# The last scattered output tile of an attention–Fourier–FFN kernel: one store of 768 columns, or two of 384

## The chip, the cores and the metric

The kernel runs on one core of a Trainium2 chip. The metric is device time in microseconds (us) for one execution of the whole program. Engines are named by their role: TensorE (PE in the profile, with its weight loads as PEld), VectorE (DVE), ScalarE (ACT), GpSimd (POOL) and SyncE (SP). DMA transfers are issued from SyncE's queue and from GpSimd's queue, and all run on the same 16 DMA engines.

## The reference

Attention with normalised queries and keys, then a Fourier mix, a layer norm and a feed-forward block, for 8 batches of 448 rows and 768 columns:

```python
batch, n_heads, seq, head_dim = (8, 12, 448, 64)
...
scores = np.matmul(q_n, k_n.transpose(0, 1, 3, 2)) / tau
attn = np.exp(scores - max); attn = attn / sum
x = np.matmul(attn, v)            # heads side by side: (8, 448, 768)
...
X = np.fft.fft(np.fft.fft(x, axis=1), axis=2)
u = x + np.real(X)
un = (u - mu) / np.sqrt(var + 1e-06)
ch = np.maximum(un @ w_ch1, 0.0) @ w_ch2        # 768 -> 3072 -> 768
return (u + ch).astype(np.float32)
```

The output is float32: one row is 768 numbers, 3 KB.

## The kernel before

The program is written as a list of operations (`Plan.add`), each with its engine, an estimated duration, a priority, and the names of what it reads and writes. A list scheduler (`Plan.schedule`) puts them into one fixed order for each engine, and `Plan.emit` writes that order out with the semaphore waits that the reads and writes need. Two rules of `emit` matter here. On GpSimd each instruction waits for the semaphore of the instruction before it, and an indirect store raises that semaphore too (`engine_sem`). An instruction that must wait for a transfer waits for that transfer's own semaphore, `st0`, `st1`, `st1z` for the direct stores from SyncE and `sx0`, `sx1` for the indirect stores from GpSimd. At the end SyncE waits for all of these, and then every engine drains and they meet in a barrier (line L1571 in the profile).

The 448 rows of a batch are held in tiles of 128 rows (`utiles`): A0 has rows in their natural order, A1 has mirrored rows, Yt has rows 128 and on with a mirrored piece, and Zt collects 64 mirrored rows of an even batch and 64 of the odd batch after it. A0 is stored by a direct DMA from SyncE (L1378). The other tiles go to rows that are not evenly spaced, so GpSimd stores them by an indirect DMA (L1386) that takes the 128 row numbers from a column of the table `IDX` ([128, 8 batches, 3 kinds of tile], int32). `IDX` is filled once, at the start of the program, by `iota` instructions on GpSimd (L551 to L556). The column of kind 2 (Zt) is used for the odd batches alone.

`ffn(b)` computes the second matrix product and the stores. It takes two row tiles u0 and u1 at a time, and gets the four output halves (two tiles by two halves of 384 columns) from seven products m1 to m7 of 12 matmuls each. For the last batch (`last_b`) the second pair is u0 = Zt, with output buffer 0, and u1 = A0, with buffer 1. In order of time on the engines:

- m1: ScalarE copies it from PSUM into half 0 of buffer 0 (L1352), GpSimd adds the residual tile to it in two instructions of 192 columns (L1357).
- m2: VectorE adds it from PSUM to half 0 of buffer 0 (L1364, called `fin{i}0`): half 0 of u0 is complete.
- m6, m5: copied by ScalarE and added to by GpSimd in the same way, into half 1 of buffer 0 and half 1 of buffer 1 (two pairs of L1357).
- m7: VectorE completes half 1 of u1 (L1364); SyncE stores it. VectorE also prepares the last 128 columns of u1 (L1464), which the next products wait for.
- m3: VectorE completes half 1 of u0 (L1364, `fin{i}1`); then GpSimd stores all 768 columns of u0.
- m4, in two parts of 256 and 128 columns: VectorE completes half 0 of u1 (L1364, L1470); SyncE stores it in two parts.

So the indirect store of Zt (u0) and the last direct store of A0 (u1) are the last things that leave the core.

Of the kernel before, what the change touches and what calls it, by code (L numbers as in the profile page):

```python
# [12 lines left out]
B, H, S, DH = 8, 12, 448, 64  # L13
# [394 lines left out]
def t_dve(n, mode=1):  # L408
    return 0.1 + n / (960.0 * mode)
# [15 lines left out]
class Kern:  # L425
# [943 lines left out]
    def store(self, b, i, ut, ob, c=None, c0=0, c1=384):  # L1369

        P = self.P
        A0, A1, Yt, Zt, zo = self.utiles(b)
        rd_ = [f"OUT{ob}", f"OUT{ob}b"] if c is None else [f"OUT{ob}" + "b" * c + "z" * (c0 > 0)]
        cs = slice(0, DM) if c is None else slice(384 * c + c0, 384 * c + c1)
        o = self.OUTB[:, ob, cs]
        if ut == A0:
            n = cs.stop - cs.start
            op = P.add("sp", lambda sy, sem: sy.dma_start(  # L1378
                bass.AP(self.out.tensor, b * S * DM + cs.start, [[DM, 128], [1, n]]), o).then_inc(sem, 16),
                0.36, -1, f"st{i}_{b}", reads=rd_, dma=(f"st{ob}" + "z" * (c0 > 0), 16), serve=1.2)  # L1380
            self.first_st = self.first_st or op
        else:
            w = {A1: 0, Yt: 1, Zt: 2}[ut]

            def st(g, sem, esem):
                g.indirect_dma_start(  # L1386
                    self.out.rearrange("b s d -> (b s) d"),
                    bass.IndirectOffsetOnAxis(self.IDX[:, b, w:w + 1].bitcast(mybir.dt.uint32), 0),
                    o, None, engine_sem=esem).then_inc(sem, 16)
            P.add("pool", st, 1.2, -1, f"sc_{i}_{b}", reads=rd_ + ["IDX"], dma=(f"sx{ob}", 16), serve=1.2)  # L1390

    def ffn(self, b):
        P = self.P
        tiles = self.tiles(b)
        HH = NF // 2
        if b == 0:
            self.up(0, (0,), range(0, NF, 4), False)
            self.up(0, (1, 2), range(0, NF, 2), True)
            for i, ut in enumerate(tiles):
                ob = self.out_next % 2  # L1400
# [23 lines left out]
        def comb(o, a, bq, k, op, nm):  # L1424
            cs = lambda q: self.HQ[:, q, 4 * k:4 * k + 4, :].rearrange("p f c -> p (f c)")
            rd = sorted(set(hr(a)(k) + hr(bq)(k)))
            P.add("dve", lambda v: v.tensor_tensor(cs(o), cs(a), cs(bq), op), 0.46, -0.5, f"{nm}{k}_{b}", reads=rd, writes=hr(o)(k))  # L1427
        last_b = b == self.nb - 1
        for i, two in ((0, 0), (1, 1)) if b == self.nb - 2 else [(i, i + 1 < len(tiles)) for i in range(0, len(tiles), 2)]:
            if two:  # L1430
                u0, u1 = tiles[i], tiles[i + 1]
                if b >= self.nb - 2:
                    if not last_b:
                        self.wsum3()
                    self.ups(b, (i, i + 1))
                else:
                    self.up(b, (i, i + 1), chunks, True)
                for k in range(3):
                    comb(4, 2, 3, k, AluOp.add, "s1")
                    comb(2, 2, 0, k, AluOp.subtract, "s3")  # L1440
                b1, ta, tb = Tile("M"), Tile("M"), Tile("G" if last_b else "M")
                op = self.prod(b, b1, H(0), W(0, 0), hr(0), wr(0), f"m1{i}", True, False)
                rd = self.fin(b, b1, op, 0, 0, u0, "a", f"fa{i}")
                for k in range(3):
                    comb(0, 4, 0, k, AluOp.subtract, "s2")
                op = self.prod(b, ta, H(1), W(1, 0), hr(1), wr(1), f"m2{i}", True, True)
                self.fin(b, ta, op, 0, 0, u0, "out", f"fin{i}0")
                for k in range(3):
                    comb(1, 1, 0, k, AluOp.subtract, "s4")
                op = self.prod(b, b1, H(0), TT(1), hr(0), tr(2), f"m6{i}", False, False, rd)  # L1450
                rd = self.fin(b, b1, op, 0, 1, u0, "a", f"fv{i}")
                op = self.prod(b, tb, H(4), TT(0), hr(4), tr(1), f"m5{i}", True, False)
                rd2 = self.fin(b, tb, op, 1, 1, u1, "a", f"fm{i}")
                op = self.prod(b, b1, H(2), W(0, 1), hr(2), tr(3), f"m7{i}", False, False, rd)
                m7 = op
                rd = self.fin(b, b1, op, 1, 1, u1, "out", f"fin{i + 1}1")
                if last_b and i + 2 == len(tiles):
                    self.store(b, i + 1, u1, 1, 1)
                op = self.prod(b, tb, H(1), W(1, 1), hr(1), wr(1), f"m3{i}", False, True, rd2)
                self.fin(b, tb, op, 0, 1, u0, "out", f"fin{i}1")  # L1460
                self.store(b, i, u0, 0)
                if last_b and i + 2 == len(tiles):
                    tz, cz = Tile("G"), slice(256, 384)
                    pre = P.add("dve", lambda v: v.tensor_tensor(self.OUTB[:, 1, cz], self.PS[:, self.bank(b1), cz], self.U[:, u1, cz], AluOp.add), t_dve(128), -1,  # L1464
                                f"finz_{b}", reads=self.unames(b, u1), writes=["OUT1z"], after=(m7,), tiles=(b1,))
                    op = self.prod(b, b1, H(3), lambda f: self.TX[:, 2, f, 0:256], hr(3), tr(4), f"m4{i}", False, True, rd, n=256, more=[pre])
                    self.fin(b, b1, op, 1, 0, u1, "u", f"fin{i + 1}0", 0, 256)
                    self.store(b, i + 1, u1, 1, 0, 0, 256)
                    op = self.prod(b, tz, H(3), lambda f: self.TX[:, 2, f, cz], hr(3), tr(4), f"m4{i}", True, True, n=128)
                    P.add("dve", lambda v: v.tensor_tensor(self.OUTB[:, 1, cz], self.PS[:, self.bank(tz), 0:128], self.OUTB[:, 1, cz], AluOp.add), t_dve(128), -1,  # L1470
                          f"finz_{b}", reads=["OUT1z"], writes=["OUT1z"], after=(op,), tiles=(tz,))
                    self.store(b, i + 1, u1, 1, 0, 256, 384)
                    continue
                op = self.prod(b, b1, H(3), TT(2), hr(3), tr(4), f"m4{i}", False, True, rd)
                self.fin(b, b1, op, 1, 0, u1, "u", f"fin{i + 1}0")
                self.store(b, i + 1, u1, 1)
                continue
            u0 = tiles[i]
            self.up(b, (i,), (0, 12, 4, 16, 8, 20), False)
            for k in range(3):  # L1480
                comb(4, 0, 2, k, AluOp.add, "s5")
            for c, ((q0, r0, n0, w0), (q1, r1, n1, w1)) in enumerate((((0, W(0, 0), "y0", wr(0)), (2, W(1, 0), "y1", wr(1))),
                                                                 ((0, W(0, 1), "y2", tr(3)), (4, W(1, 1), "y3", wr(1))))):
                tile = Tile("M")
                self.prod(b, tile, H(q0), r0, hr(q0), w0, f"{n0}{i}", True, False)
                op = self.prod(b, tile, H(q1), r1, hr(q1), w1, f"{n1}{i}", False, True)
                self.fin(b, tile, op, 0, c, u0, "u", f"fin{i}{c}")
            self.store(b, i, u0, 0)
# [136 lines left out]
```

## Time and profile before

| | us |
|---|---|
| median of 3 runs | 580.69 |
| lowest and highest of them | 579.79, 581.12 |
| the profiled execution, its own time | 579.86 |
| its span, first to last instruction | 578.1 |
| last matmul of TensorE ends | 573.64 |
| last indirect store: issue on GpSimd, start and duration | 573.03, 0.99 |

All rows below come from the profiled execution, with times from the start of its span. In a timeline row the two numbers are start and duration of an instruction (or of several in a row, xN), then engine, source line, operation and out<-in; what stands in brackets is the idle time of the engine before it and who ended it. A "q" after an engine's name marks its queue of instructions that only wait or issue. In the chain of waits each row has a start, a length and what the chain ran through then.

### The profile page before, as it was taken

The page shows a single profiled execution, that of the slowest core. Times are in us where ns is not written, and L with a number is a line of the kernel's source. Part 1 is how long each engine was busy: PE and PEld are TensorE (multiplying, and loading weights), DVE is VectorE, ACT ScalarE, POOL GpSimd, SP SyncE. Part 2 cuts the span into 40 slices and gives each one's busy share as a digit, 9 for nine tenths or more (in the row PEclk, how much of TensorE's full clock was granted, in tenths as well). Part 3 has the DMA queues.
Part 4 walks back from the last instruction along what each step waited for, and adds up shares of the span by engine and source line. Part 5 has one row for each costly group of instructions (what it writes and reads, how often), then busy time and mean ns, then how long its engine had stood idle before and what let it go on. Part 6 is the DMA issues. An engine that isn't in the chain of part 4 may idle for free.

```text
span 578.1 us, 15943 instructions
## 1 busy us (share of the span) xinstructions
PE 561.2 (97%) x6496; PEld 442.3 (77%) x6496; DVE 427.6 (74%) x1066; ACT 391.8 (68%) x764; POOL 208.2 (36%) x318
## 2 busy tenths in 40 slices
PE   3889999999999999999999999999999999999996
PEld 3679887686697786878687687878778687969684
DVE  8889878886688788866768477865877486967262
ACT  8897885568975685687747676488647743847170
POOL 8635324544372525533260525413180210030302
PEclk9999999999999999999999999999999999999999
DMA  9999999892597719952592429833591110021101
GB/s 214 178 231 171 155 176 182 169 176 45 125 145 95 178 35 139 169 111 61 114 157 47 93 76 160 149 69 87 91 115 47 28 57 28 17 56 43 45 13 55
DMA packets 187787, 62.19 MB, mean 108 GB/s; under 512 B 166721, under 2 KB 185537, under 8 KB 187713
## 3 DMA queue, kind: packets, MB, share of 16 engines
q1 hardware_dynamic: 129792, 38.35, 35.1%
q0 software_dynamic: 57920, 22.81, 32.1%
q8 instruction: 51, 0.84, 0.6%
q14 instruction: 24, 0.19, 0.1%
HBM read 51.90 MB, written 11.01 MB: 109 GB/s over the span
## 4 chain that ended last, share of the span: by engine, by line
PE 92%; DVE 3%; POOL 2%; issue 1%; ACT 1%; POOLq 0%
PE PS L1332 34%; PE PS L1188 30%; PE PS L1283 7%; PE PS L926 6%; PE PS L889 5%; PE PS L1013 2%; PE PS L920 2%; PE PS L1051 2%; PE PS L901 1%; PE PS L902 1%; PE PS L1564 1%; PE PS L744 1%; POOL VB L847 1%; DVE X L946 1%; ACT E L867 0%
## 5 line engine op out<-in xcount | busy, mean ns | idle before, releaser
L1188 PE MATMUL PS<-UNT,W1b 128*128 128x256 bf16 (+1 forms) x1872 | 187.9, 256 | 0.0
L1188 PEld LDWEIGHTS PS<-UNT,W1b 128*128 128x128 bf16 x1872 | 156.2, 98 | 18.8 <-issue 4.1
L867 ACT ACTIVATE E<-PS 128x900 bf16<-128x900 f32 (+1 forms) x192 | 148.8, 829 | 27.6 <-PE PS L889 25.6
L1332 PE MATMUL PS<-W2b,HQ 128*128 128x384 bf16 x768 | 133.3, 326 | 0.0
L1332 PEld LDWEIGHTS PS<-W2b,HQ 128*128 128x128 bf16 x768 | 73.9, 98 | 45.4 <-issue 0.9
L815 POOL TENSOR_TENSOR QH<-STG,SM 128x256 bf16<-128x256 f32 x126 | 79.1, 656 | 81.4 <-DVE SM L624 71.6
L1357 POOL TENSOR_TENSOR OUTB<-OUTB,U 128x192 f32<-128x192 f32 x66 | 37.6, 591 | 169.5 <-ACT OUTB L1352 169.1
L1204 ACT ACTIVATE HQ<-PS 128x512 bf16<-128x512 f32 x83 | 49.6, 597 | 42.9 <-PE PS L1188 42.5
L1332 PE MATMUL PS<-TX,HQ 128*128 128x384 bf16 (+2 forms) x408 | 71.0, 321 | 0.0
L1427 DVE TENSOR_TENSOR HQ<-HQ 128x512 bf16<-128x512 bf16 x141 | 60.4, 454 | 13.8 <-ACT HQ L1204 7.7
L1332 PEld LDWEIGHTS PS<-TX,HQ 128*128 128x128 bf16 x408 | 38.4, 98 | 23.5 <-issue 1.1
L926 PE MATMUL PS<-VB,E 128*128 128x65 bf16 x1152 | 51.2, 193 | 0.0
L926 PEld LDWEIGHTS PS<-VB,E 128*128 128x128 bf16 x1152 | 47.6, 97 | 1.2
L806 ACT ACTIVATE QH<-STG 128x384 f32<-128x384 f32 x84 | 42.5, 521 | 7.9 <-DVE SM L808 5.0
L808 DVE TENSOR_REDUCE SM<-QH 128x6 f32<-128x384 f32 x84 | 44.2, 539 | 4.6 <-ACT QH L806 4.4
L1204 DVE TENSOR_SCALAR HQ<-PS 128x512 bf16<-128x512 f32 x43 | 29.7, 691 | 21.3 <-PE PS L1188 21.1
L920 PE MATMUL PS<-VZ,E 128*128 128x130 bf16 x192 | 41.6, 219 | 0.3 <-DVE X L946 0.3
L1386 POOL DMA_INDIRECT out_dram<-OUTB,IDX x20 | 21.3, 1064 | 54.8 <-DVE OUTB L1364 27.5
L889 PE MATMUL PS<-QK 64*128 64x225 bf16 x576 | 39.6, 259 | 0.6 <-ACT E L867 0.3
L1079 DVE SCALAR_TENSOR_TENSOR U<-ACG,X 128x384 bf16<-128x384 f32 (+3 forms) x70 | 39.4, 583 | 0.9
L1352 ACT ACTIVATE OUTB<-PS 128x384 f32<-128x384 f32 x33 | 16.2, 492 | 30.4 <-PE PS L1332 30.3
L946 DVE TENSOR_TENSOR X<-PS,RD 128x512 bf16<-128x512 f32 (+1 forms) x49 | 33.1, 678 | 1.2
(176 smaller groups left out, 792.7 us busy)
## 6 DMA issues: line engine op xcount, KB each, us to landing
STG<-in_k_dram SPq DMA_DIRECT2D x18, 384.0 KB, 3.9
STG<-in_q_dram SPq DMA_DIRECT2D x18, 384.0 KB, 3.7
VB<-in_v_dram POOLq DMA_DIRECT2D x24, 192.0 KB, 6.1
W1b<-in_moe_w_ch_dram POOLq DMA_DIRECT2D x12, 384.0 KB, 7.0
W2b<-in_moe_w_ch_dram POOLq DMA_DIRECT2D x12, 384.0 KB, 6.7
out_dram<-OUTB SPq DMA_DIRECT2D x7, 384.0 KB
TX<-in_k_dram SPq DMA_DIRECT2D x2, 576.0 KB, 5.6
TX<-in_q_dram SPq DMA_DIRECT2D x2, 576.0 KB, 6.0
```

What stands on the lines that cost most here:

```text
L806: P.add("act", lambda a, sq=sq, src=buf[:, w * x:w * x + w]: a.activation(sq, src, ACTF.Square), t_act(w), pr, f"sq{i}_{b}", reads=bn, wri ...
L808: P.add("dve", lambda v, o=SS[:, i, H // ns * x:H // ns * (x + 1)], sq=sq: v.tensor_reduce(o, sq.rearrange("p (h d) -> p h d", d=DH), AX.X ...
L815: r = v.tensor_tensor(v3(qh)[:, h:h + 4], v3(buf)[:, h:h + 4], RN[:, i, h:h + 4].unsqueeze(2).to_broadcast((128, 4, DH)), AluOp.mult)
L867: return a.activation(o, self.PS[:, bk:bk + nc_, 0:SQ2], ACTF.Exp, scale=1.0 / self.tau)
L889: i = pe.matmul(self.PS[:, bk + h, c0:c0 + NK], self.KT[r, jj, kt * 128:(kt + 1) * 128], self.QT[r, jj, cols], start=True, stop=True)
L920: r = pe.matmul(o, st(6), self.VZ[:, j, :], start=not split, stop=(split and i == 0), skip_group_check=True)
L926: r = pe.matmul(o[:, 65 * h:65 * h + 65], st(2 * kt + h), self.VB[:, kt, 2 * j + h, :], start=(split and i == h == kt == 0), stop=((not sp ...
L1188: r = pe.matmul(self.PS[:, bk, x * n:(x + 1) * n], self.W1b[:, j, ft * 128:(ft + 1) * 128], self.UNT[:, j, cs], start=(j == 0), stop=(j == ...
L1204: return e.activation(o, i, ACTF.Relu) if e is self.nc.scalar else e.tensor_relu(o, i)
L1283: r = pe.matmul(o[:, 128 * f:128 * f + 128], lhs(j, n * g + f), rhs[:, j, :], start=(start and j == 0 and f == 0), stop=(stop and j == 2 a ...
L1332: r = pe.matmul(self.PS[:, bk, 0:n], lhs(f), rhs(f), start=(start and f == 0), stop=(stop and f == NF // 2 - 1), skip_group_check=True)
L1427: P.add("dve", lambda v: v.tensor_tensor(cs(o), cs(a), cs(bq), op), 0.46, -0.5, f"{nm}{k}_{b}", reads=rd, writes=hr(o)(k))
```

## The change

The store of the last batch's Zt tile is written as two stores. `store` for columns 0 to 383 is placed right after `fin{i}0`, and the store at the old place sends columns 384 to 767 alone. For these two the output is seen as rows of 384 columns, so that row r of the output becomes rows 2r and 2r + 1, and the index columns hold 2r for the first half and 2r + 1 for the second. They stand in `IDX[:, 0, 2:3]` and `IDX[:, 2, 2:3]`, which belong to the even batches 0 and 2 and are not used otherwise. Four `iota` instructions on GpSimd (64 partitions each) write them at the start of the last batch's `ffn`. The halves use the semaphores `sx0` and `sx1`.

```diff
             def st(g, sem, esem):
                 g.indirect_dma_start(
-                    self.out.rearrange("b s d -> (b s) d"),
-                    bass.IndirectOffsetOnAxis(self.IDX[:, b, w:w + 1].bitcast(mybir.dt.uint32), 0),
+                    self.out.rearrange("b s d -> (b s) d") if c is None else self.out.rearrange("b s (h d) -> (b s h) d", h=2),
+                    bass.IndirectOffsetOnAxis((self.IDX[:, b, w:w + 1] if c is None else self.IDX[:, 2 * c, 2:3]).bitcast(mybir.dt.uint32), 0),
                     o, None, engine_sem=esem).then_inc(sem, 16)
-            P.add("pool", st, 1.2, -1, f"sc_{i}_{b}", reads=rd_ + ["IDX"], dma=(f"sx{ob}", 16), serve=1.2)
+            P.add("pool", st, 1.2, -1, f"sc_{i}_{b}", reads=rd_ + ["IDX"], dma=(f"sx{ob}" if c is None else f"sx{c}", 16), serve=1.2)
...
         last_b = b == self.nb - 1
+        if last_b:
+            for c in range(2):
+                for x in range(2):
+                    P.add("pool", lambda g, c=c, x=x: g.iota(self.IDX[64 * x:64 * x + 64, 2 * c, 2:3], [[0, 1]], base=2 * (320 + (b - 1 + x) * S) + c, channel_multiplier=-2),
+                          0.16, -2, f"iz{c}{x}", writes=["IDX"])
...
                 self.fin(b, ta, op, 0, 0, u0, "out", f"fin{i}0")
+                if last_b and i + 2 == len(tiles):
+                    self.store(b, i, u0, 0, 0)
...
                 self.fin(b, tb, op, 0, 1, u0, "out", f"fin{i}1")
-                self.store(b, i, u0, 0)
+                self.store(b, i, u0, 0, 1 if last_b and i + 2 == len(tiles) else None)
```

The order of instructions on TensorE, VectorE, ScalarE and SyncE is the same as before. On GpSimd the four index writes come after batch 6's two indirect stores and ahead of the last batch's first additions; the first half's issue comes after m1's pair of additions and ahead of those of m6 and m5; the second half's issue is last, where the whole tile's issue was.

## The prediction

> **What bounds the kernel now.** I read the page first, then the end of the chain of waits, because the change touches only the last pair of row tiles of the last batch.
>
> ```profile
> span 578.1 us, 15943 instructions
> PE 561.2 (97%) x6496; PEld 442.3 (77%) x6496; DVE 427.6 (74%) x1066; ACT 391.8 (68%) x764; POOL 208.2 (36%) x318
> PE 92%; DVE 3%; POOL 2%; issue 1%; ACT 1%; POOLq 0%
> ```
>
> TensorE is busy for 97% of the span and makes up 92% of the chain that ended last. Nothing in the change adds or removes a matmul, so all that it can win lies behind the last matmuls. The chain of waits at the end, in order of time:
>
> ```profile
> 559.96 11.71 PE PS L1332 x72
> ...
> 571.70 0.57 DVE OUTB L1364
> 572.27 0.03 POOLq L383
> ...
> 572.81 1.21 POOLq L1571
> ```
>
> The chain leaves TensorE at 571.67, takes the addition of the tile's second half (L1364) and goes to GpSimd. The timeline of that stretch shows what surrounds it:
>
> ```profile
> 563.92 0.56 DVE L1364 TENSOR_TENSOR OUTB<-PS,OUTB 128x384 f32<-128x384 f32 x1 [0.51 <-PE PS L1332]
> ...
> 566.42 1.05 POOL L1357 TENSOR_TENSOR OUTB<-OUTB,U 128x192 f32<-128x192 f32 x2 [2.60 <-ACT OUTB L1352]
> ...
> 568.37 1.05 POOL L1357 TENSOR_TENSOR OUTB<-OUTB,U 128x192 f32<-128x192 f32 x2 [0.90 <-ACT OUTB L1352]
> 569.75 0.56 DVE L1364 TENSOR_TENSOR OUTB<-PS,OUTB 128x384 f32<-128x384 f32 x1 [4.61 <-PE PS L1332]
> 570.22 0.28 DVE L1464 TENSOR_TENSOR OUTB<-PS,U 128x128 f32<-128x128 f32 x1
> 570.34 4.00 SPq L1378 DMA_DIRECT2D out_dram<-OUTB  x3
> ...
> 571.50 2.14 PE L1332 MATMUL PS<-TX,HQ 128*128 128x256 bf16 x24
> 571.70 0.56 DVE L1364 TENSOR_TENSOR OUTB<-PS,OUTB 128x384 f32<-128x384 f32 x1 [1.20 <-PE PS L1332]
> 573.03 0.99 POOL L1386 DMA_INDIRECT out_dram<-OUTB,IDX  x1 [3.61 <-DVE OUTB L1364]
> ...
> 573.68 0.29 DVE L1470 TENSOR_TENSOR OUTB<-PS,OUTB 128x128 f32<-128x128 f32 x1 [0.18 <-PE PS L1332]
> ```
>
> The first half of the tile is ready at 564.48 (563.92 + 0.56), the second at 572.26. The one issue (L1386) for both runs from 573.03 to 574.02. Beside it the last tile's direct stores leave SyncE; the third is released by the addition that ends at 573.97, and its issue ends at 574.34 (570.34 + 4.00). So two stores end the kernel, on different queues, at nearly the same moment. SyncE's own waits after 574 us show how they end:
>
> ```profile
> SPq L397 <- DMA out_dram<-OUTB,IDX: 2.4, 1, 2.4
> SPq L1571 <- PEq L1571: 0.8, 1, 0.8
> SPq L397 <- DMA out_dram<-OUTB: 0.2, 1, 0.2
> ```
>
> And the instructions of the closing line L1571, with their durations in ns:
>
> ```profile
> L1571 POOLq DRAIN x1: 5020/5020/5020, 572.8 to 572.8; - x1
> ...
> L1571 SPq DRAIN x1: 13/13/13, 577.2 to 577.2; - x1
> ```
>
> SyncE waits 2.4 us for the indirect store, then only 0.2 us more for the last direct one. It is done at 577.2 and then sits 0.8 us in the closing barrier. The wait is put down to TensorE, which has long finished; the engine still at work is GpSimd, whose drain began at 572.8 and took 5.02 us, to 577.8. The span ends 0.2 us later. The end therefore hangs on GpSimd's drain, and next behind it, 0.6 us earlier, on the landings that SyncE awaits.
>
> **The change part by part.**
>
> *Four index writes.* They rewrite two index columns and wait for both of batch 6's indirect stores to land. Nearest rows: the longest index write of the start (among the groups), the queue around their new place, and all indirect stores with their landing.
>
> ```profile
> L555 POOL IOTA IDX<- 64x8 int32 x1 | 0.5, 458 | 0.1
> ```
> ```profile
> 519.71 0.97 POOL L1386 DMA_INDIRECT out_dram<-OUTB,IDX  x1 [1.62 <-DVE F L1120]
> 534.87 1.23 POOL L1357 TENSOR_TENSOR OUTB<-OUTB,U 128x192 f32<-128x192 f32 x2 [14.19 <-ACT OUTB L1352]
> ```
> ```profile
> L1386 POOL DMA_INDIRECT out_dram<-OUTB,IDX x20: 972/1040/1424, 111.2 to 573.0; - x20
> DMA to landing us min/median/max: 3.0/3.9/5.6
> ```
>
> With the slowest landing, 519.71 + 5.6 = 525.3; four writes at 0.46 + 0.1 us end by 527.6. What is queued behind them on GpSimd is the addition at 534.87, which waits for ScalarE. Cost 0; 7.3 us of cover. Without that cover it would be 2.2 us of queue.
>
> *The first half's issue, moved ahead of two pairs of additions on GpSimd (L1357).* It is released at 564.48. From the chain's 572.27 to the issue's start at 573.03 are 0.76 us, so it starts at 565.24 and runs 0.99, at most 1.42 us: to 566.23, at most 566.66. The pair at 566.42 starts then or up to 0.24 us late. Its reader is the addition at 571.70, so that lateness is free. The next pair starts at 568.37 on ScalarE's release; the pair before it would end by 567.7, so it does not move. Cost 0. The cover ends where the issue lasts over about 2 us: then the pair at 568.37 is late, its reader at 569.75 after 0.3 us of slack, and after 1 us more (570.50 to 571.50) the matmuls. Its transfer falls in a stretch without other stores until 570.34.
>
> *The second half's issue.* Still released by the addition at 572.26. Does half the width halve its 0.99 us? No row has an indirect issue of another width, so I take the bounds from direct issues on GpSimd:
>
> ```profile
> L847 POOL DMA_DIRECT2D VB<-in_v_dram x24: 1017/1052/1271, 8.9 to 419.5; - x24
> ...
> L602 POOL DMA_DIRECT2D W2b<-in_moe_w_ch_dram x12: 696/710/762, 52.3 to 83.1; - x12
> ```
>
> L847 issues 192 KB in 128 x 12 short runs and takes 1.05 us; L602 issues 384 KB in few long runs and takes 0.71. The issue goes by runs, not bytes, and the half tile still has 128 rows. I take no change; bounds are half of it (-0.49) and the slowest issue seen (1.42, so +0.43).
>
> *The second half's transfer: the one real gain.* The DMA queues between 574 and 577 us (packets, MB, share of 16 engines' time), the last two issues with their landing, and the DMA share (next to last column) in steps of 0.4 us:
>
> ```profile
> q0 software_dynamic: 80, 0.39, 31.5%
> q1 hardware_dynamic: 288, 0.20, 20.8%
> ...
> out_dram<-OUTB SPq DMA_DIRECT2D x1, 64.0 KB, 2.9
> out_dram<-OUTB,IDX POOLq DMA_INDIRECT x1, 3.7
> ```
> ```profile
> 574.40:574.80 0.40, 0.00 (x0) 0.00 (x0) 0.00 (x0) 0.00 (x0) 0.00 (x0) 1.00 1.06 382
> 574.80:575.20 0.40, 0.00 (x0) 0.00 (x0) 0.00 (x0) 0.00 (x0) 0.00 (x0) 1.00 1.01 399
> 575.20:575.60 0.40, 0.00 (x0) 0.00 (x0) 0.00 (x0) 0.00 (x0) 0.00 (x0) 1.00 0.90 372
> ```
>
> The engines are full from 574.4 to 575.6 with both queues, so both stores end late because they share. The indirect one takes 31.5% of 3 us = 0.945 us of every engine; half of it is 0.47 us, and both landings should come that much earlier: the indirect from 573.03 + 3.7 = 576.7 to 576.3, the last direct one from 576.9 (573.97 + 2.9) to 576.4. The direct one cannot hold the end up by itself: its 64 KB are a third of q1's bytes, and a third of q1's 0.62 us (20.8% of 3 us) is 0.2 us of each engine. Bounds: 0, if latency and not the full engines sets the landing, and the whole half, -0.47. I take -0.47, as the share stands at 0.9 to 1.06 while both run.
>
> The page DMA: Bandwidth & Descriptors of the Trainium skill, section Bandwidth, tabulates 0.95 us of engine time for 64 KB and 6.15 us for 1 MB; by that slope 192 KB less would be worth an estimated 1.04 us, and the sum -1.04. The table is for loads; this trace has 0.39 MB of store in 0.945 us, and I stay with it. The same page, section Rules for kernel authors, speaks against the change: coalesce transfers, since each pays its overhead again; here that second overhead would fall between 565 and 571 us, in time nothing waits for.
>
> *GpSimd's drain.* It ends 1.1 us after the indirect landing (576.7 to 577.8) and 3.8 us after the issue's end (574.02). If it waits for the transfer, it moves with it: -0.47. If it counts from the issue, it does not: 0. I take the first, because the drain outlasts any work the engine shows.
>
> Sum: 0 + 0 + 0 - 0.47 = -0.47 us. The profiled execution took 579.86 us (span 578.1 and 1.8 around it), so 579.4; the three runs before have a median of 580.69, 0.83 above it, which gives 580.2.
>
> **The rivals.**
>
> *The drain counts from the issue* (or the second issue is as slow as 1.42 us, which cancels the gain): 580.7. For it: 0.8 us of SyncE's waiting already stands behind the drain. Against it: nothing but the drain's length.
>
> *More goes than the transfer.* The issue halves with the bytes (-0.49 - 0.47 = -0.96, 579.7), or the drain also loses the 0.6 us by which it outlasts SyncE (-1.07, 579.6); both together 579.1. Against: L602 and L847 as read above.
>
> *GpSimd is held by the first half until it lands* (slower). The next instruction on GpSimd waits for the issue's semaphore; were that to come at landing, 565.24 + 3.9 = 569.1, at most 570.8. Both pairs then run one behind the other, the second ending 2.1 us later at 571.3 to 573.0; its reader (569.75) is 1.5 to 3.3 us late, and after 1 us of slack the last matmuls by 0.5 to 2.3 us. With the transfer's gain that is 580.7 to 582.5; it costs more than it brings from a landing of 3.8 us on, and 0.2% from about 4.9. Against it: two issues in a row before, though the first took over 3 us to land:
>
> ```profile
> 545.32 0.99 POOL L1386 DMA_INDIRECT out_dram<-OUTB,IDX  x1 [3.56 <-DVE OUTB L1364]
> 547.08 0.97 POOL L1386 DMA_INDIRECT out_dram<-OUTB,IDX  x1 [0.77 <-DVE OUTB L1364]
> ```
>
> The second starts 0.77 us after the first's issue ends.
>
> **How the numbers follow.** Forecast 0.52, no gain 0.22, more 0.18, held 0.08. The runs of before lie within -0.9 and +0.4 us of their median, so 0.2% (1.16 us) is about what can be told from no change. "More" crosses that bound in about half of its cases, the forecast in an eighth with the scatter of the readings: 0.09 + 0.07, faster 0.16. Slower is the worse part of "held" and a little scatter: 0.07. Range: from the middle of "more" with scatter (579.6 - 0.4) to no gain with scatter (580.7 + 0.5): 579.2 to 581.2.
>
> **What would show it.** Right: two L1386 issues, the first near 565.2 and done before 566.7; the additions at 568.37 and 569.75 and the matmuls at 571.50 unmoved; the second issue at 573.0 lasting about 0.99; q0's share after 574 halved; SyncE's drain at 576.7 and GpSimd's at 577.3. Wrong: a late pair at 568.37, a shorter or longer second issue, a drain still at 577.8, or any difference ahead of 564 us.

## The result, and the profile after

| | before | after |
|---|---|---|
| median of 22 runs each, side by side, us | 579.86 | 578.47 |
| ratio after / before, 95% interval | | 0.9974 [0.9962, 0.9986] |
| profiled execution, us | 579.86 | 578.52 |
| its span, us | 578.06 | 576.71 |
| last matmul ends, us | 573.64 | 573.90 |
| from there to the end of the span ("the tail"), us | 4.41 | 2.81 |

The kernel became 1.39 us faster by the medians, 1.34 by the spans. All of it lies behind the last matmul: the stretch ahead is 0.26 us longer, the tail 1.60 us shorter. The change was forecast to be worth 0.47 us. One of the 22 runs of after took 648.18 us at a granted clock of 0.851, against 0.997 and more in the others; the ratio leaves it out.

The page of after, span and engines:

```profile
span 576.7 us, 15950 instructions
PE 562.2 (97%) x6496; PEld 443.3 (77%) x6496; DVE 428.6 (74%) x1066; ACT 391.4 (68%) x764; POOL 210.7 (37%) x323
```

Seven instructions more than before, all on GpSimd: the four index writes and the additional issue (x318 to x323), and two that only wait. The chain of waits of after at the end, with start, length and what it ran through:

```profile
560.22 13.69 PE PS L1332 x96
573.91 0.02 issue
573.94 0.29 DVE OUTB L1477
```

In before the chain left TensorE at 571.67 for the addition that completes Zt, a queue wait (L383) and GpSimd. Now it stays on TensorE up to the last matmul. The timeline of after in the same stretch:

```profile
564.16 0.56 DVE L1364 TENSOR_TENSOR OUTB<-PS,OUTB 128x384 f32<-128x384 f32 x1 [0.55 <-PE PS L1332]
565.00 0.99 POOL L1386 DMA_INDIRECT out_dram<-OUTB,IDX  x1 [0.98 <-DVE OUTB L1364]
...
566.69 1.05 POOL L1357 TENSOR_TENSOR OUTB<-OUTB,U 128x192 f32<-128x192 f32 x2 [0.70 <-ACT OUTB L1352]
...
568.63 1.05 POOL L1357 TENSOR_TENSOR OUTB<-OUTB,U 128x192 f32<-128x192 f32 x2 [0.89 <-ACT OUTB L1352]
570.01 0.56 DVE L1364 TENSOR_TENSOR OUTB<-PS,OUTB 128x384 f32<-128x384 f32 x1 [4.56 <-PE PS L1332]
...
571.76 2.14 PE L1332 MATMUL PS<-TX,HQ 128*128 128x256 bf16 x24
571.96 0.56 DVE L1364 TENSOR_TENSOR OUTB<-PS,OUTB 128x384 f32<-128x384 f32 x1 [1.20 <-PE PS L1332]
572.79 0.99 POOL L1386 DMA_INDIRECT out_dram<-OUTB,IDX  x1 [3.12 <-DVE OUTB L1364]
```

Everything on VectorE, TensorE and GpSimd stands 0.19 to 0.27 us later than in before, much as the last matmul does (0.26). The last issue alone stands 0.24 us earlier than in before: it starts 0.28 us behind its addition (571.96 + 0.56 to 572.79, from unrounded times), where before had 0.77 (572.26 to 573.03). The first half's issue, too, starts 0.28 us behind its addition (564.72 to 565.00).

The closing line of after (durations in ns) ends GpSimd's drain at 576.5 and SyncE's at 576.2:

```profile
L1578 POOLq DRAIN x1: 3922/3922/3922, 572.6 to 572.6; - x1
...
L1578 SPq DRAIN x1: 13/13/13, 576.2 to 576.2; - x1
```

And the DMA queues of after between 574 and 577 us (packets, MB, share of 16 engines):

```profile
q1 hardware_dynamic: 288, 0.20, 20.1%
q0 software_dynamic: 64, 0.20, 16.1%
```

The indirect queue takes 16.1% of 3 us, 0.48 us of every engine, where it took 0.945. The drain, though, ends 1.35 us earlier, not 0.47. So something else moved as well, and it has to stand between the addition and the landing.

### The profile page after: what moved, and what is told of

The parts are those of the page before. It is cut to its first block, busy times and chain, and to the rows that moved or that the text cites. A ratio compares the mean times of both kernels' runs of the same rounds, so it can differ in the third digit from the quotient of the medians.

```text
span 576.7 us, 15950 instructions
## 1 busy us (share of the span) xinstructions
PE 562.2 (97%) x6496; PEld 443.3 (77%) x6496; DVE 428.6 (74%) x1066; ACT 391.4 (68%) x764; POOL 210.7 (37%) x323
## 4 chain that ended last, share of the span: by engine, by line
PE 94%; DVE 3%; POOL 2%; issue 1%; POOLq 0%
PE PS L1332 34%; PE PS L1188 31%; PE PS L1283 7%; PE PS L926 6%; PE PS L889 6%; PE PS L1013 2%; PE PS L920 2%; PE PS L1051 2%; PE PS L744 1%; PE PS L1571 1%; PE PS L901 1%; PE PS L902 1%; POOL VB L847 1%; DVE X L946 1%; DVE SM L679 1%
## 5 line engine op out<-in xcount | busy, mean ns | idle before, releaser
L926 PE MATMUL PS<-VB,E 128*128 128x65 bf16 x1152 | 51.2, 193 | 0.0
L1386 POOL DMA_INDIRECT out_dram<-OUTB,IDX x21 | 22.9, 1092 | 53.2 <-DVE OUTB L1364 36.4
```

The lines of the kernel that those rows point to most:

```text
L926: r = pe.matmul(o[:, 65 * h:65 * h + 65], st(2 * kt + h), self.VB[:, kt, 2 * j + h, :], start=(split and i == h == kt == 0), stop=((not sp ...
```

## The experiments

Three differences between the two traces could each hold a part of the 1.60 us: the bytes of the last store; the shorter way from the addition to the issue; and an instruction fetch, a single 8 KB packet on queue 14, that comes at another place. The fetch is seen in the DMA queues. Before, from 573.7 to 574.6 us:

```profile
q14 instruction: 1, 0.01, 4.2%
```

After, from 573.0 to 573.6 us:

```profile
q14 instruction: 1, 0.01, 4.7%
```

The shares are of 16 engines: 4.2% of 0.9 us times 16 is 0.60 us on one engine, 4.7% of 0.6 us times 16 is 0.45. In before it starts 0.50 us behind the end of the last matmul and runs into the last stores. In after it starts 0.79 us ahead of that end, before any packet of the last three stores.

All twelve kernels in one table, two of them run again at its end. "Wait" is the time from the end of the addition that completes Zt to the start of the last indirect issue. "Landing" is the last of the 16 semaphore increments of that store, counted from the end of the last matmul, and "fetch" the start of the 8 KB packet on the same scale. Each tail, wait, landing and fetch is from one profiled execution.

| kernel | wait | fetch | landing | tail | median / before beside it | ratio [95%] |
|---|---|---|---|---|---|---|
| before | 0.77 | +0.50 | 3.11 | 4.41 | | |
| after | 0.28 | -0.79 | 1.46 | 2.81 | 578.47 / 579.86 | 0.9974 [0.9962, 0.9986] |
| whole_apart | 0.81 | +0.50 | 2.92 | 4.23 | 580.13 / 580.31 | 1.0 [0.9992, 1.0009] |
| whole_carried | 0.28 | +0.49 | 2.94 | 4.24 | 580.23 / 580.31 | 0.9996 [0.9987, 1.0005] |
| halves_apart | 0.81 | -0.79 | 2.22 | 3.57 | 579.61 / 580.31 | 0.9991 [0.9982, 0.9999] |
| halves_carried | 0.28 | -0.80 | 1.48 | 2.83 | 578.80 / 580.31 | 0.9974 [0.996, 0.9989] |
| whole_carried_index | 0.28 | -0.79 | 1.90 | 3.21 | 578.98 / 579.89 | 0.9988 [0.9978, 0.9997] |
| second_half_only | 0.28 | -0.79 | 1.45 | 2.76 | 578.93 / 579.89 | 0.9988 [0.9973, 1.0003] |
| halves_latest_carried | 0.28 | -0.80 | 1.46 | 2.81 | 578.12 / 579.89 | 0.9963 [0.9951, 0.9976] |
| whole_apart_index | 0.81 | -0.80 | 2.65 | 3.96 | 580.05 / 579.97 | 1.0007 [0.9993, 1.0021] |
| whole_carried_pad1 | 0.28 | -0.78 | 1.92 | 3.23 | 579.47 / 579.97 | a single run |
| whole_carried_pad24 | 0.28 | -0.78 | 1.91 | 3.22 | 579.1 / 579.97 | a single run |
| carried_again | 0.28 | -0.80 | 1.46 | 2.81 | 578.51 / 580.16 | 0.997 [0.9958, 0.9982] |
| latest_again | 0.28 | -0.79 | 1.46 | 2.81 | 578.17 / 580.16 | 0.9969 [0.9957, 0.9981] |

### Where the wait stands: apart from the issue, or carried by it

An instruction that has several waits carries the one that is written first; the others become wait instructions of their own ahead of it, as the two pairs of kernels below show. `emit` writes the waits of an instruction in the order in which it meets a Python set of operations, and that order is no part of the source. In the profiled before, the wait for VectorE became an instruction of its own: it is the queue wait L383 in the chain. In the profiled after, the issue carries it. Two kernels fix the order for before, with the whole store. In whole_carried:

```diff
                         need[key] = max(need.get(key, 0), val)
                     if e == "pool" and last[0]:
                         need[("e", e)] = last[0]
+                    if op.name == "sc_2_7":
+                        need = dict(sorted(need.items(), key=lambda kv: kv[0] != ("e", "dve")))
                     for key, val in need.items():
```

whole_apart has `==` in place of `!=`.

> The kernel before, with the wait for VectorE's addition fixed in a separate wait instruction ahead of the last indirect issue. Measured as the tail: from the last matmul's end to the end of the span (before 578.06 - 573.64 = 4.4 us, after 576.71 - 573.90 = 2.8 us), and from the addition's end to the issue's start (before 0.77, after 0.28 us). Theory (two causes: where the wait stands, and half the bytes): addition to issue 0.73 to 0.77, tail 4.4 us, time as before. Rival (half the bytes do it all, the wait's place is without effect): the same.

> The kernel before, with that wait fixed in the indirect issue itself. Theory: addition to issue 0.28, tail shorter by 0.45 us or more (3.9 us or less), time 0.45 us or more under the other whole one. Rival: addition to issue 0.28 to 0.77, but tail 4.4 us, because the direct stores' transfers and the drain end it anyway.

Two more fix it for after. halves_carried:

```diff
+                    if op.name == "sc_2_7" and op.dma[0] == "sx1":
+                        need = dict(sorted(need.items(), key=lambda kv: kv[0] != ("e", "dve")))
                     for key, val in need.items():
```

and halves_apart with `==`.

> The changed kernel, with the wait for the second half's addition fixed in a separate instruction ahead of its issue. Theory: addition to issue 0.73 to 0.77; tail between 3.25 us (2.8 + 0.45) and 3.9 us (4.4 less the 0.47 us predicted for half the bytes). Rival: tail 2.8 us, as in the changed kernel.

> The changed kernel, with that wait fixed in the issue itself, as the profiled build of it had it by chance. Both: addition to issue 0.28 us, tail 2.8 us. The theory has it 0.45 us or more ahead of the halves with the wait apart; the rival has the two alike.

The chain of waits of halves_apart shows what the separate wait costs:

```profile
571.49 0.57 DVE OUTB L1366
572.06 0.02 issue
572.08 0.04 POOLq L385
572.12 0.51 issue
```

The addition is over at 572.06 and the wait instruction at 572.12. Then GpSimd's sequencer needs 0.51 us more, in which it waits for nothing that the profile shows. The issue in the timelines of halves_apart and of halves_carried, with GpSimd's idle time ahead of it in brackets:

```profile
572.86 0.99 POOL L1388 DMA_INDIRECT out_dram<-OUTB,IDX  x1 [3.65 <-DVE OUTB L1366]
```
```profile
573.33 0.98 POOL L1388 DMA_INDIRECT out_dram<-OUTB,IDX  x1 [3.12 <-DVE OUTB L1366]
```

3.65 against 3.12 us idle for the same release: 0.53 us. The last matmuls end at 573.43 and 574.44 in these two executions, so the issue stands 0.57 ahead of that end in the one and 1.11 in the other. In the halves the tail follows: 3.57 us apart, 2.83 carried, the latter as in after (2.81). In the whole store it doesn't: 4.23 apart, 4.24 carried, where 3.9 or less had been expected. The start of the issue alone therefore does not explain the difference between before and after. The landings say more than the tails: carried, fifteen of the sixteen come 0.77 us earlier (the fifteenth at 1.94, apart at 2.71), and the sixteenth does not (2.94 and 2.92). GpSimd's closing drains agree with the tails. halves_apart, then halves_carried:

```profile
L1580 POOLq DRAIN x1: 4142/4142/4142, 572.6 to 572.6; - x1
```
```profile
L1580 POOLq DRAIN x1: 3937/3937/3937, 573.1 to 573.1; - x1
```

They end at 576.8 and 577.0, that is 3.34 and 2.60 us behind the last matmul. In all fourteen traces the drain's end lies 1.08 to 1.12 us behind the last landing of the indirect store. The last direct store always lands later than that one (in after at 2.01, against 1.46), and yet SyncE, which waits for both, always ends ahead of the drain, by 0.26 to 0.63 us.

### What the four index writes do by themselves

The halves differ from the whole store by more than the store: they have the index writes. whole_carried_index is whole_carried with the change's four index writes alone, which nothing reads; whole_apart_index is whole_apart with the same lines.

```diff
         last_b = b == self.nb - 1
+        if last_b:
+            for c in range(2):
+                for x in range(2):
+                    P.add("pool", lambda g, c=c, x=x: g.iota(self.IDX[64 * x:64 * x + 64, 2 * c, 2:3], [[0, 1]], base=2 * (320 + (b - 1 + x) * S) + c, channel_multiplier=-2),
+                          0.16, -2, f"iz{c}{x}", writes=["IDX"])
```

> The kernel before with the wait carried by the issue, and the change's four index writes alone added (to columns that nothing then reads); one whole store. In whole_carried 15 of the 16 landings of the last indirect store came by 1.94 us after the last matmul and the 16th at 2.94: an 8 KB instruction fetch, 0.49 us after the last matmul, holds one DMA engine (q14 in the DMA view). In the halves it came 0.80 us ahead of the last matmul, before the stores. Theory A (the fetch is moved by the number of GpSimd instructions, and moving it is part of the change's gain): the fetch comes ahead of the last matmul, the 16th landing at about 2.0, tail about 3.3 us and 0.9 us faster than whole_carried. Theory B (the fetch moves with the halved store, or by chance): fetch at +0.49, tail 4.2 us, time as before.

> The kernel before with the wait in a separate instruction and the four index writes added: whole_apart with only the fetch moved. Theory (the fetch moves ahead of the last matmul and then holds no engine): the landings of the indirect store by 2.7 us after the last matmul without a straggler, tail about 4.05 us (whole_apart 4.23), and from here to halves_apart (3.57) the halved transfer is worth 0.47, the predicted term. Rival (the halves bring more than their bytes): tail 4.2, or over 0.6 us from here to halves_apart.

Four instructions of 124 ns that run some fifty microseconds before the end, with nothing waiting for them, take 1.03 us from the tail of the whole store with the wait carried (4.24 to 3.21) and 0.27 with the wait apart (4.23 to 3.96). The fetch tells how. whole_carried, DMA queues from 574.6 to 575.5 us, while the indirect store fills the engines:

```profile
q0 software_dynamic: 60, 0.37, 102.4%
q14 instruction: 1, 0.01, 5.2%
```

5.2% of 0.9 us times 16 is 0.75 us of one engine, in the middle of the store. whole_carried_index has the fetch between 573.2 and 574.0 us, alone on the engines and ahead of the last matmul's end at 574.10:

```profile
q14 instruction: 1, 0.01, 4.1%
```

whole_carried in stretches (the last two columns are the DMA share and GB/s):

```profile
574.60:575.60 1.00, 0.00 (x0) 0.00 (x0) 0.00 (x0) 0.00 (x0) 0.00 (x0) 1.00 0.99 385
575.60:576.20 0.60, 0.00 (x0) 0.00 (x0) 0.00 (x0) 0.00 (x0) 0.00 (x0) 1.00 0.97 319
576.20:576.60 0.40, 0.00 (x0) 0.00 (x0) 0.00 (x0) 0.00 (x0) 0.00 (x0) 1.00 0.07 24
576.60:577.20 0.60, 0.00 (x0) 0.00 (x0) 0.00 (x0) 0.00 (x0) 0.00 (x0) 1.00 0.06 20
```

whole_carried_index, whose last matmul ends within 0.1 us of the other's:

```profile
576.20:576.60 0.40, 0.00 (x0) 0.00 (x0) 0.00 (x0) 0.00 (x0) 0.00 (x0) 1.00 0.00 0
```

A share of 0.06 to 0.07 is one engine of 16: nearly all are done at 576.2, and about one works on for a microsecond. The landings agree. In whole_carried the fifteenth comes 1.94 us behind the last matmul and the sixteenth at 2.94; in whole_carried_index they come at 1.88 and 1.90. What waits for this store waits for the slowest of its engines. That the late engine is the one that fetched is inferred from this: the packets of the trace do not say on which engine they ran.

Is it the index writes, or their number? whole_carried_pad1 and whole_carried_pad24 add one and 24 index writes to an unused column:

```diff
+        for x in range(1) if last_b else ():
+            P.add("pool", lambda g: g.iota(self.IDX[0:64, 4, 2:3], [[0, 1]], base=0, channel_multiplier=0), 0.16, -2, "izp", writes=["IDX"])
```

> whole_carried with one index write of no use instead of four, at the same place. If any added instruction on GpSimd moves the fetch: fetch near -0.8 us, tail 3.2. If it takes a certain count (a boundary in the instruction stream): fetch still at +0.49, tail 4.2.

> whole_carried with 24 index writes of no use on GpSimd (24 x 0.19 = 4.6 us of queue between 524 and 535 us, in which it waits). If the fetch's place goes with the count of GpSimd's instructions, it moves further ahead than -0.8 us, or another fetch takes its place; tail 3.2 us where no fetch falls between -0.1 and 2.5 us after the last matmul. If it takes two places alone: -0.8 or +0.49 again.

One instruction does what four and 24 do: the fetch at -0.78, the tail at 3.23 and 3.22. So the fetch has been seen at two places only, and any instruction added to GpSimd in these kernels put it at the early one. The fetch before it on queue 14 moved too, from 36.4 us ahead of the last matmul's end without an added instruction to 48.7 with one index write and 50.6 to 51.2 in the others. Which engine's instructions the last one brings, and why one instruction on GpSimd moves it, was not settled.

By the medians, whole_carried_index gains 0.91 us on the before beside it and whole_carried 0.08, which roughly agrees with their tails (1.20 and 0.17 us below that of before), though the intervals of the two ratios overlap. whole_apart_index does not: its tail is 0.45 us below that of before and its ratio is 1.0007 with an interval down to 0.9993, 0.4 us. The small share of the fetch with the wait apart is thus read from single profiles and not confirmed by times.

### Does the first half's store cost anything

second_half_only is halves_carried without the first half's store; columns 0 to 383 of the last Zt tile are not stored.

```diff
-                if last_b and i + 2 == len(tiles):
-                    self.store(b, i, u0, 0, 0)
```

> The changed kernel with the wait carried by the issue, and without the first half's store: columns 0 to 383 of the last Zt tile are not stored. Theory (the first half's issue and transfer are hidden): tail 2.8 us as in halves_carried, the additions on GpSimd at 566.4 to 568.4 as in the kernel before, time within 0.1% of halves_carried. Rival (the first half costs something on GpSimd or in the DMA engines): tail or the stretch ahead of it shorter by over 0.2 us.

Its tail is 2.76 us against 2.83 with the first half's store, landing 1.45 against 1.48, and its ratio 0.9988 [0.9973, 1.0003] overlaps that of halves_carried. The first half's issue and transfer cost nothing that the times can tell. Of the 0.06 us of tail, 0.04 is in the drain: it ends 1.08 us behind the landing here and in the kernels with the whole store, and 1.12 in those with both halves.

### The latest wait carried everywhere

If a carried wait is worth half a microsecond at the end, it might be worth something at every instruction. halves_latest_carried sorts the waits of every instruction on every engine by the planned end of what they wait for, the latest first:

```diff
+                        due[key] = max(due.get(key, 0.0), d.end)
...
+                        due[("e", e)] = last[1].end
+                    need = dict(sorted(need.items(), key=lambda kv: -due[kv[0]]))
                     for key, val in need.items():
```

> The changed kernel with the waits of every instruction on every engine put in an order: the one that the plan expects last is carried by the instruction itself, the others stand in wait instructions ahead of it. Theory (where the last wait stands matters at the kernel's end alone, since TensorE bounds the rest): as halves_carried, tail 2.8 us, 0.9974 of before, within 0.1%. Rival (late waits in separate instructions cost along the whole kernel): faster than halves_carried by over 1 us.

It gave 0.9963 [0.9951, 0.9976]. Beside halves_carried, repeated as carried_again, it was repeated as latest_again:

> halves_carried once more, beside the next one on the same chip. Both theories: tail 2.8 us, 0.997 to 0.998 of before.

> halves_latest_carried once more. It had 0.9963 of before, halves_carried 0.9974 in another call. Theory (the place of the last wait counts at the end alone): within 0.1% of the one beside it. Rival (it counts along the kernel): faster than it by over 0.1%, with the last matmul ending earlier by over 0.5 us.

0.997 and 0.9969: no difference that the intervals can tell (0.34 us by the medians). The second sign of the rival, a last matmul that ends over 0.5 us earlier, did show in the traces: 573.50 and 572.94 us, against 574.44 and 574.95 in halves_carried and its repetition. But the profiled execution of carried_again was the slowest of its six (579.57) and that of latest_again the fastest of its six (577.59), so the sign is no evidence by itself. A gain along the kernel of some tenths of a microsecond is thus neither shown nor excluded. No version is shown to be faster than the change with the wait of its last issue carried, about 0.997 of before, and the profiled after is already one.

## Why the prediction was wrong

It named the right stage, and its one gain, the halved transfer, was sized about right (0.47 us forecast, 0.38 to 0.39 measured). What failed are two terms that it put at nothing: the start of the second issue, which it took as fixed, and the index writes, which moved an instruction fetch out of the last stores. With both, the tail lost another 1.2 us. By the medians the forecast was short by 0.92 us of gain (1.39 - 0.47), besides a base that was 0.83 us high; 578.47 lies 0.73 us below its range. Its rival "more goes than the transfer" came nearest in size, but by none of its ways: the issue did not get shorter, and the drain still ends last, 0.30 us behind SyncE's (576.48 and 576.18), where before had 0.62. The rival in which GpSimd is held by the first half fell: the next pair starts 0.70 us behind that issue's end (565.99 to 566.69), released by ScalarE. By its own steps:

- **What bounds the end.** Right. In every kernel the end hangs on GpSimd's drain, and the drain follows the last landing of the indirect store by 1.08 to 1.12 us.
- **The drain waits for the transfer.** Right. From the issue's end to the drain's end are 3.81 us in before and 2.70 in after; the rival that counts from the issue falls.
- **Index writes.** The queue was read rightly. They run at 523.91, 0.70 us for the four, and the next work on GpSimd starts at 535.12. Their timeline in after:

```profile
523.91 0.70 POOL L1432 IOTA IDX<- 64x1 int32 x4 [3.58 <-DMA out_dram<-OUTB,IDX]
535.12 1.24 POOL L1357 TENSOR_TENSOR OUTB<-OUTB,U 128x192 f32<-128x192 f32 x2 [10.51 <-ACT OUTB L1352]
```

  The cost of 0 holds for that queue, but not for the kernel: this is one of the two steps that failed. Their presence moved the fetch, which was a gain of 0.27 us of tail with the wait apart and 1.03 with it carried. The prediction had not looked at queue 14 although its packet lay in the very stretch that it read. So it took the landing at 576.7 for the end of a full transfer, where fifteen landings of before had come by 2.70 us behind the last matmul and only the sixteenth at 3.11.
- **The first half's issue.** Right. It starts at 565.00, earlier than the 565.24 forecast, is over before the pair at 566.69, and holds nothing up.
- **The length of the second issue.** Right: 0.99 us, for half the bytes.
- **The start of the second issue.** This is the other step that failed. The prediction took "From the chain's 572.27 to the issue's start at 573.03 are 0.76 us" as a fixed way and put both issues that far behind their additions. The measured way is 0.28 us where the issue carries the wait and 0.77 to 0.81 where it doesn't. The trace of before had shown both. Its timeline has, ahead of the issue at 545.32 which the prediction quotes, an addition that ends 0.78 us before it, and at another place one that ends 0.28 before:

```profile
388.63 0.56 DVE L1364 TENSOR_TENSOR OUTB<-PS,U 128x384 f32<-128x384 f32 x1 [2.83 <-PE PS L1332]
...
389.47 1.04 POOL L1386 DMA_INDIRECT out_dram<-OUTB,IDX  x1 [10.34 <-DVE OUTB L1364]
...
543.98 0.56 DVE L1364 TENSOR_TENSOR OUTB<-PS,OUTB 128x384 f32<-128x384 f32 x1 [1.39 <-PE PS L1332]
```

  388.63 + 0.56 to 389.47 is 0.28 us. With two values in sight, 0.5 us belonged among the bounds, on the side of a gain. That after would get the shorter one was luck: nothing in the change asks for it.
- **The halved transfer.** Right in kind and size: forecast 0.47. With wait and fetch held equal, the halves' tail is 0.39 us shorter with the wait apart (3.96 to 3.57) and 0.38 with it carried (3.21 to 2.83); the landing comes 0.43 and 0.42 us earlier. The slope of the Trainium skill's table (DMA: Bandwidth & Descriptors, section Bandwidth) had made an estimated 1.04 us of it; these runs disagree, with 0.4. The rule of the same page of the Trainium skill to coalesce transfers (section Rules for kernel authors) names an overhead that these runs do not show in the time, as the tail of second_half_only is only 0.06 us shorter.
- **The base.** The prediction added its gain to the median of three runs, 580.69. The 22 runs of before have 579.86, which is also what the profiled execution took.

The tails add up along one path: fetch early 4.41 to 3.96, wait carried 3.96 to 3.21, half the bytes 3.21 to 2.83, together 1.58 us of the 1.60 measured. Of the first step, 0.18 us already lies between before and whole_apart (4.41 and 4.23), which both have the wait apart and the fetch late; their sixteenth landing comes 0.41 and 0.21 us behind the fifteenth. The first two steps can't be priced alone. With the fetch late, carrying the wait brings nothing (4.23, 4.24): the fifteen landings come earlier and the sixteenth does not. With the fetch early it brings 0.75, of which 0.53 is the issue's own start. The rest probably belongs to the order of packets: with the wait carried, the indirect store lands at 1.90, ahead of the last two direct ones (2.26 and 2.44), and with it apart at 2.65, between them (1.51 and 2.86). Halves with the fetch at its late place were not run. All these sizes are read from tails of single profiles, which repeat within 0.02 us where a kernel with an early fetch was profiled again; the times, with intervals of 0.1% (0.6 us) or more to either side, do not separate neighbours on this path.

How much of the 1.39 us is owed to the change's idea? halves_apart against whole_apart_index gives the bytes alone, 0.39 us of tail. By the times, halves_apart is at 0.9991 [0.9982, 0.9999] of before: the change, without the wait's better place, is at most barely told from nothing. The rest came with the new program, through instructions added on GpSimd, of which one is enough to move the fetch, and through an order of waits that the source doesn't fix. Neither was meant by the change.

The 0.26 us ahead of the last matmul is within the scatter. Over the fourteen traces of the table that end lies between 572.94 and 574.95 us, and halves_carried and its repetition are 0.51 apart (574.44 and 574.95) with tails of 2.83 and 2.81.

## What to carry to other kernels

At the end of a kernel, compare the tail (from the last matmul on) and not the whole span: here it repeats within 0.02 us between equal kernels with an early fetch, where their span scatters by a microsecond (576.71 to 577.76). Look which of an instruction's waits it carries, and let the last one on the path to the end be that one. And before a gap is taken as a constant, look for the same gap at other places of the trace; before a gain is put down to an edit, hold fixed what any edit may move, the fetches and the order of the waits.

## What the runs showed of the hardware that was not expected

- A wait instruction ahead of an indirect issue on GpSimd cost 0.5 us more than the same wait carried by the issue: 0.77 to 0.81 us from the addition to the issue, against 0.28 in the ten traces where the issue carries it.
- One 8 KB instruction fetch, 0.32 to 0.75 us on one of the 16 DMA engines, goes with a last landing that is held back by up to 1.0 us (1.94 to 2.94 in whole_carried), where it falls among the last stores. The Trainium skill (Runtime: NRT & Kernel Launch, section Instruction fetch mechanics) calls the cost of such a fetch mostly hidden; these traces agree where the fetch starts 0.8 us ahead of the last matmul's end (sixteenth landing 0.01 to 0.04 us behind the fifteenth), and not where it starts 0.5 us behind it (0.21 to 0.99 us).
- Fetches can move by a microsecond when an instruction is added on GpSimd far from them, to the same place for one, four and 24 added index writes and for the whole change (-0.78 to -0.80 us from the last matmul's end, where it was +0.49 to +0.50).
